# LSH attention with two gated layers: the first layer's weight rests all on GpSimd, two preparation parts a step at the start

## The chip, the cores and the metric

The kernel runs on one core of one Trainium2 chip. The metric is the device time of one execution in microseconds (us), median of several. The five engines are named as in the profile: PE (TensorE matmul; PEld its weight loads), DVE (VectorE), ACT (ScalarE), POOL (GpSimd), SP (SyncE, which here issues most DMAs).

## The reference

The computation is a masked attention, then two feed-forward layers, in fp32:

```
q_bits = (q @ proj > 0);  k_bits = (k @ proj > 0)          # 6 hash bits a token
mask   = bucket(q)[:, None] == bucket(k)[None, :]
scores = where(mask, scale * q @ k.T, -1e9)                # 2 batches, 8 heads, 768 tokens, 64 columns
x      = softmax(scores) @ v                               # -> (1536, 512)
x      = (silu(x @ w_gate) * (x @ w_val)) @ w_out          # first layer, d_ff 1536
h      = x @ w_in
out    = (max(h, 0) + alpha * min(h, 0)) @ w_out2          # second layer, d_ff 2048
```

The weights arrive as 64-bit numbers (raw blocks of 128x512, 512 KB each).

## The kernel before

**Precision.** Every operand of the layers is held as two rounded parts, a head (h) and a rest (l), and a product is three matmuls (lines 608 to 610). For a weight block this means: load the raw block (line 489, DMA issued by SP), make an fp32 block `wt` from it (`round64`: line 506 on ACT, 507 and 509 on DVE, 511 on POOL), round it to the head in `wb` (`w_h`, line 546, ACT), and subtract the head to get the rest (`w_l`, line 553). The rest of block i is made on POOL where i is even and on DVE where i is odd (`PL = (2, 1)`). The first layer has 36 blocks (24 of w_gate and w_val, 12 of w_out); they are new only in the first pass and are put into a scratch in DRAM after it (`w_put`, line 557, SP), from which later passes load both parts ready. So line 553 works for the first layer 36 times, 18 on each engine. The buffers of this pipeline: raw 2, `wr` 2, `wt` 3, `wb` 5.

**Attention.** It is cut into 24 items: a batch, a pair of heads, and a group of 256 queries. An item has two units, one per head. A unit goes through four parts: `banks` (score matmuls, lines 280 and 281, and their evacuation, 282), `top` (the maximum over keys, lines 286 to 289, and a transpose), `back` (the maximum broadcast, subtraction on DVE, line 307, and exponential on ACT, line 312) and `values` (matmuls of line 319). A unit yields 8 times, an item 16 times. Behind every one of these small pieces `step()` (line 380) pops one part from the list `todo`. The list holds the preparation of the next items (`prep`, line 223): for the first item of a pair of heads the rests of the keys (line 175, head 0 on POOL, head 1 on DVE), rounding of the queries (180) and their rest (183, POOL), two hashes of the keys and one of the queries. A hash is four matmuls (191, 192), the bits (197, DVE) and two copies into the operands (203, ACT). All hashes of the start pass through one PSUM tile `hp` and one SBUF tile `mk`. Before a unit's banks the list is emptied by force until its item is ready (line 435).

**Order.** At the start the attention runs alone until the first four items (one group of queries of all four head pairs) are done (line 791); in this time the loads and the first conversions of weights are called from `prime`. Then the pass `stage1(0)` of the first layer over these 256 tokens runs with the attention of the next group between its blocks, at two pieces per yield, and so on for three more groups; then a pass over 512 tokens, then three passes of the second layer. The lines of the source are a priority: the framework that places the instructions lets one whose inputs it takes to be late stand behind later ones, so the order on an engine is read from the trace.

```
        def step():
            if todo:
                todo.pop(0)()
...
            n, m = PL
            eng = nc.gpsimd if i % n < m else nc.vector
```

Of the kernel before, what the change touches and what calls it, by code (L numbers as in the profile page):

```python
# [46 lines left out]
def lsh_attention_moe_kernel(  # L47
# [12 lines left out]
    nc = tc.nc  # L60
# [8 lines left out]
    NPAIR = H // 2  # L69
# [11 lines left out]
    def f32(ap):  # L81
        return ap.bitcast(F32)
# [45 lines left out]
    at = Bag()  # L128
# [20 lines left out]
    def load_v(it):  # L149

        t = at.sm.tile([P, NC, 3 * D], F32, tag="vv", name="vv", bufs=4)
        VV[it.b, it.p] = t
        nc.gpsimd.memset(t[:, :, D:2 * D], 1.0)
        for x in range(2):
            nc.sync.dma_start(out=t[:, :, 2 * x * D:(2 * x + 1) * D], in_=vP[it.b, 2 * it.p + x])

    def load_k(it):

        if it.b == 0:
            it.nat = wp.tile([P, S], F32, tag="raw64", name="nat", bufs=RAWB)  # L160
        else:
            it.nat = at.sm.tile([P, S], F32, tag="nat", name="nat", bufs=1)
        nc.sync.dma_start(out=it.nat, in_=kview2(it))
        nc.gpsimd.dma_start(out=KA(it)[0:D], in_=kview(it))
        nc.gpsimd.dma_start(out=KB(it)[0:D], in_=kview(it))

    def load_q(it, eng=nc.sync):
        it.qr = at.sm.tile([P, 2, GQ], F32, tag="qr", name="qr", bufs=2)
        eng.dma_start(out=it.qr, in_=qview(it))
# [53 lines left out]
    def prep(it):  # L223

        def rest():
            pass

        todo = []
        if it.first:
            todo += [lambda x=x: rest_k(it, x, nc.gpsimd if POOL_K[x] else nc.vector) for x in range(2)]  # L230
        if it.first and it.b > 0:
            todo += [lambda: load_v(it)]
        todo += [lambda: round_q(it), lambda: rest_q(it)] + [rest] * (1 if it.first else 4)
        if it.first:
            todo += hash_k(it, 0) + hash_k(it, 1)
        todo += hash_q(it)
        last = todo[-1]

        def end():
            last()  # L240
            it.ready = True

        todo[-1] = end
        return todo

    def load(it):
        if it.first and it.b > 0:
            load_k(it)
        load_q(it)
# [7 lines left out]
    def first_item(it):  # L257
        ka, kb = KA(it), KB(it)
        for x in range(2):
            nc.scalar.activation(out=ka[0:D, x], in_=it.nat[x * D:(x + 1) * D, :], func=AF.Copy)  # L260
        round_q(it)
        for x in range(2):
            rest_k(it, x, nc.vector)
        nc.vector.tensor_tensor(out=it.QB[0:D], in0=it.qr[0:D], in1=f32(it.QA)[0:D], op=ALU.subtract)
        for x in range(2):
            nc.scalar.activation(out=kb[0:D, x], in_=it.nat[x * D:(x + 1) * D, :], func=AF.Copy)
        for fn in hash_q(it) + hash_k(it, 0, "G") + hash_k(it, 1, "G"):
            fn()
        it.ready = True

    def s_bank(u, j):
        it = u.it
        if j == 0:
            u.se = at.sm.tile([P, NC, GQ], F32, tag="se", name="se", bufs=at.nse)
        pt = at.ps.tile([P, 2, GQ], F32, tag=at.tag["S"][j], name="S", bufs=at.nb[at.tag["S"][j]])
        qa, qb = it.QA[:, u.x, :], it.QB[0:KR, u.x, :]
        ka, kb = KA(it)[:, u.x, :], KB(it)[0:KR, u.x, :]
        for i in range(2):
            sl = slice((2 * j + i) * P, (2 * j + i + 1) * P)
            nc.tensor.matmul(pt[:, i, :], lhsT=ka[:, sl], rhs=qa, start=True, stop=False)  # L280
            nc.tensor.matmul(pt[:, i, :], lhsT=kb[:, sl], rhs=qb, start=False, stop=True)  # L281
        nc.scalar.activation(out=u.se[:, 2 * j:2 * j + 2, :], in_=pt, func=AF.Copy)  # L282

    def s_max(u):
        m2 = at.sm.tile([P, 2, GQ], F32, tag="m2", name="m2", bufs=1)
        nc.vector.tensor_tensor(out=m2, in0=u.se[:, 0:2, :], in1=u.se[:, 2:4, :], op=ALU.max)
        nc.vector.scalar_tensor_tensor(out=m2, in0=u.se[:, 4:6, :], scalar=FLOOR, in1=m2, op0=ALU.max, op1=ALU.max)
        u.m1 = at.sm.tile([P, GQ], F32, tag="m1", name="m1", bufs=1)
        nc.vector.tensor_tensor(out=u.m1, in0=m2[:, 0, :], in1=m2[:, 1, :], op=ALU.max)

    def s_mt(u):

        tp = at.ps.tile([P, 2, P], F32, tag=at.tag["m"], name="mt", bufs=at.nb[at.tag["m"]])
        for j in range(2):
            nc.tensor.transpose(tp[:, j, :], u.m1[:, j * P:(j + 1) * P], ident)
        u.mq = at.sm.tile([P, 2, 1], F32, tag="mq", name="mq", bufs=2)
        nc.vector.tensor_reduce(out=u.mq, in_=tp, axis=AX.X, op=ALU.max)

    def s_mb(u):
        bc = at.ps.tile([P, 2, P], F32, tag=at.tag["m"], name="mb", bufs=at.nb[at.tag["m"]])  # L300
        for j in range(2):
            nc.tensor.transpose(bc[:, j, :], u.mq[:, j, :].to_broadcast([P, P]), ident)  # L302
        u.mx = bc.rearrange("p a b -> p (a b)")
# [7 lines left out]
    def s_exp(u):  # L311
        nc.scalar.activation(out=u.se, in_=u.se, func=AF.Exp, scale=SCALE)  # L312
# [39 lines left out]
    for b in range(B):  # L352
        order = [(p, g) for g in range(NG) for p in range(NPAIR)]
        for p, g in order:
# [3 lines left out]
            it.first = not any((o.b, o.p) == (b, p) for o in items)  # L358
            items.append(it)
    at.done = 0  # L360

    def attention():

        us = []
        for it in items:
            for x in range(2):
                u = Bag()
                u.it, u.x = it, x
                us.append(u)
        todo = []  # L370

        def queue(i):

            if i + 2 < len(items):
                todo.extend(prep(items[i + 2]))
            if i + 3 < len(items):
                n = 2 if items[i + 2].first and i > 0 else 1
                todo.insert(min(len(todo), n), lambda: load(items[i + 3]))

        def step():  # L380
            if todo:
                todo.pop(0)()

        load_k(items[1])
        load_q(items[1])
        load_v(items[0])
        first_item(items[0])
        for i in (2, 3):
            load_k(items[i])
            load_v(items[i - 1])  # L390
        load_q(items[2])
        load_v(items[3])
        todo.extend(prep(items[1]))

        def banks(u):
            for j in range(3):
                s_bank(u, j)
                step()
                yield
            if u.x == 1:  # L400
                queue(u.it.i)

        def top(u):
            s_max(u)
            s_mt(u)
            step()
            yield

        def back(u):
            s_mb(u)  # L410
            s_sub(u)
            s_exp(u)
            step()
            yield

        def values(u):
            for j in range(3):
                s_pv(u, j)
                if j == 2 and u.x == 1:
                    s_den(u.it)  # L420
                    s_out(u.it)
                    s_xh(u.it)
                    s_xl(u.it)
                step()
                yield

        order = []
        for i, u in enumerate(us):
            for k, part in enumerate((banks, top, back, values)):
                slot = i + LAGS[k]  # L430
                order.append(((slot, i, k) if slot < OLDER else (slot, k, i), part, u))
        order.sort(key=lambda o: o[0])
        for _, part, u in order:
            if part is banks:
                while not u.it.ready:
                    todo.pop(0)()
            yield from part(u)
# [3 lines left out]
    F2I = 3 * F1  # L441
# [27 lines left out]
    seq = order1() * (len(RATES) + 1) + o2 * NP2  # L469
# [78 lines left out]
    def w_l(i):  # L548

        if new[i]:  # L550
            n, m = PL
            eng = nc.gpsimd if i % n < m else nc.vector
            eng.tensor_tensor(out=ready[i][:, 1, :], in0=wt.pop(i), in1=f32(ready[i])[:, 0, :], op=ALU.subtract)  # L553

    def w_put(i):
# [216 lines left out]
    def more():  # L772

        if next(side, 0) == 0:
            kv.close()
            return False
        return True

    def prime(k):

        if k == 60:
            setup_alpha()
        k -= PRIME[0]
        if k >= 0 and k % PRIME[1] == 0:
            i = k // PRIME[1]
            upto("load", min(i, 7), w_load)
            if i >= 4:
                upto("conv", min(i - 3, 4), w_conv)

    k = 0  # L790
    while at.done < NPAIR:
        more()
        k += 1
        prime(k)
    at.tag = dict(S="SSM", m="S", hp="S", po="po")
    early_steps = w_early()
    ws.pin = False
# [78 lines left out]
```

## Time and profile before

| | us |
|---|---|
| median of 3 runs | 916.35 |
| lowest, highest | 914.65, 919.17 |
| profiled execution, whole | 920.38 |
| its span, first to last instruction | 918.60 |

| engine | busy us in the span | share |
|---|---|---|
| PE | 845.2 | 92% |
| DVE | 570.9 | 62% |
| ACT | 441.6 | 48% |
| POOL | 377.0 | 41% |

The shares are means over stages with different limits. The span falls, by what the engines do, into the attention alone (to about 73 us, where the first weight is converted), the pass in which the 36 blocks of the first layer are converted (73 to 250 us) and the rest, where PE works almost without a pause. The profiled execution took 4.03 us more than the median of the runs.

### The profile page before, as it was taken

Reading aid. Unit: us, or ns where it says so; the run is one execution under the profiler, and the core shown is the slowest. Engines: PE = TensorE matmul, PEld = TensorE weight load, DVE = VectorE, ACT = ScalarE, POOL = GpSimd, SP = SyncE. Lnnn points to the kernel's source line nnn. Section 1 sums busy time; section 2 is a strip of 40 time slices with the busy share of each in tenths; the row PEclk is TensorE's granted clock in tenths of the full one; section 3 lists DMA queues with packets and bytes.
Section 4 is the critical chain, followed back from the end, with each engine's and each line's share of the span. In section 5 each row is a group of like instructions: output and inputs, shape, how many; then the busy total and the mean of one; then the engine's idle time right before and its main releaser. Section 6 shows DMA issues by size and latency. Waiting matters only on the chain.

```text
span 918.6 us, 13016 instructions
## 1 busy us (share of the span) xinstructions
PE 845.2 (92%) x4816; PEld 737.4 (80%) x4816; DVE 570.9 (62%) x856; ACT 441.6 (48%) x760; POOL 377.0 (41%) x327
## 2 busy tenths in 40 slices
PE   5798778677899999999999999899999999999998
PEld 3577667566789999999999987687888888888886
DVE  5689997897847766778786537564543344335432
ACT  5578566646646566565665323231433343333331
POOL 4215565666514312223221235443454445444442
PEclk9999899989999999999999999999999999999999
DMA  9424567789899756776766698887300010001001
GB/s 216 101 70 147 195 233 251 235 223 281 260 342 307 209 190 211 243 237 226 247 220 213 227 341 299 318 299 277 136 1 1 1 47 0 1 1 46 1 0 46
DMA packets 63487, 158.45 MB, mean 172 GB/s; under 512 B 18112, under 2 KB 24256, under 8 KB 63424
## 3 DMA queue, kind: packets, MB, share of 16 engines
q1 hardware_dynamic: 61264, 152.07, 49.7%
q0 software_dynamic: 2016, 5.51, 2.9%
q8 instruction: 38, 0.62, 0.3%
q14 instruction: 25, 0.20, 0.1%
q10 hardware_dynamic: 144, 0.05, 0.0%
HBM read 132.44 MB, written 25.17 MB: 172 GB/s over the span
## 4 chain that ended last, share of the span: by engine, by line
PE 69%; DVE 12%; ACT 5%; DMA 5%; POOL 5%; issue 3%; SPq 0%; POOLq 0%; DVEq 0%; ACTq 0%
PE po L319 9%; PE gp L608 6%; PE gp L609 6%; PE gp L610 6%; PE op L614 5%; PE hp L609 5%; PE op L613 5%; PE hp L608 5%; PE op L615 5%; PE hp L610 5%; DMA wb<-w 3%; POOL wt L511 3%; PE yp L610 3%; PE yp L608 3%; PE yp L609 3%
## 5 line engine op out<-in xcount | busy, mean ns | idle before, releaser
L603 POOL TENSOR_TENSOR gl<-ex,gh 128x512 fp32r<-128x512 f32 (+1 forms) x108 | 116.6, 1079 | 220.9 <-ACT gh L600 162.7
L608 PE MATMUL gp<-xh,wb 128*128 128x256 f32 (+1 forms) x480 | 155.9, 325 | 22.2 <-ACT wb L546 12.1
L610 PE MATMUL gp<-xh,wb 128*128 128x256 f32 (+1 forms) x480 | 150.6, 314 | 7.4 <-DVE wb L553 3.8
L609 PE MATMUL gp<-xl,wb 128*128 128x256 f32 (+1 forms) x480 | 148.7, 310 | 1.7 <-POOL xl L348 1.7
L319 PE MATMUL po<-se,vv 128*128 128x256 f32 x576 | 145.7, 389 | 4.8 <-ACT se L312 3.9
L608 PEld LDWEIGHTS gp<-xh,wb 128*128 128x128 f32 x480 | 93.1, 194 | 33.4 <-ACT wb L546 15.1
L319 PEld LDWEIGHTS po<-se,vv 128*128 128x128 f32 x576 | 104.6, 194 | 18.5 <-ACT se L312 5.9
L546 ACT ACTIVATE wb<-w 128x512 fp32r<-128x512 f32 x96 | 60.7, 632 | 117.8 <-PE hp L610 78.9
L600 ACT ACTIVATE gh<-ex 128x512 fp32r<-128x512 f32 (+1 forms) x108 | 57.8, 535 | 109.0 <-DVE ex L597 46.7
L553 POOL TENSOR_TENSOR wb<-w,wb 128x512 fp32r<-128x512 f32 x48 | 62.1, 1294 | 110.3 <-ACT wb L546 108.3
L610 PEld LDWEIGHTS gp<-xh,wb 128*128 128x128 f32 x480 | 93.6, 195 | 14.1 <-DVE wb L553 5.1
L312 ACT ACTIVATE se<-se 128x1536 f32<-128x1536 f32 x48 | 71.3, 1485 | 61.6 <-DVE se L307 61.4
L609 PEld LDWEIGHTS gp<-xl,wb 128*128 128x128 f32 x480 | 93.7, 195 | 6.0 <-POOL xl L348 1.9
L553 DVE TENSOR_TENSOR wb<-w,wb 128x512 fp32r<-128x512 f32 x48 | 36.4, 758 | 91.5 <-ACT wb L546 91.5
L282 ACT ACTIVATE se<-S 128x512 f32<-128x512 f32 x144 | 80.2, 593 | 22.7 <-PE S L281 19.1
L511 POOL TENSOR_TENSOR wt<-wt,wr 128x512 int32<-128x512 int32 x48 | 67.7, 1410 | 54.7 <-DVE wt L509 29.8
L307 DVE SCALAR_TENSOR_TENSOR se<-se,mb 128x1536 f32<-128x1536 f32 x48 | 83.8, 1745 | 5.0 <-PE mb L302 4.7
L280 PE MATMUL S<-QA,kt 128*128 128x256 f32 x288 | 82.9, 317 | 2.5 <-ACT se L282 2.3
L608 PE MATMUL yp<-gh,wb 128*128 128x256 f32 (+1 forms) x240 | 76.0, 318 | 7.6 <-ACT wb L546 5.7
L281 PE MATMUL S<-qb,kt 76*128 76x256 f32 x288 | 75.8, 295 | 2.4 <-ACT kt L203 2.2
L610 PE MATMUL yp<-gh,wb 128*128 128x256 f32 (+1 forms) x240 | 72.6, 308 | 4.9 <-POOL wb L553 3.4
L608 PE MATMUL hp<-xh,wb 128*128 128x512 f32 x192 | 74.7, 389 | 0.0
(94 smaller groups left out, 1852.2 us busy)
## 6 DMA issues: line engine op xcount, KB each, us to landing
wb<-w SPq DMA_DIRECT2D x144, 512.0 KB, 4.6
raw<-in_wblk_dram SPq DMA_DIRECT2D x68, 512.0 KB, 4.2
w<-wb SPq DMA_DIRECT2D x36, 512.0 KB, 4.9
qr<-in_q_dram SPq DMA_DIRECT2D x24, 256.0 KB, 3.7
kt<-in_k_dram POOLq DMA_DIRECT2D x14, 384.0 KB, 9.3
nat<-in_k_dram SPq DMA_DIRECT2D x8, 384.0 KB, 5.0
vv<-in_v_dram SPq DMA_DIRECT2D x16, 192.0 KB, 6.7
whole<-wt SPq DMA_DIRECT2D x12, 256.0 KB, 2.2
```

What stands on the lines that cost most here:

```text
L280: nc.tensor.matmul(pt[:, i, :], lhsT=ka[:, sl], rhs=qa, start=True, stop=False)
L281: nc.tensor.matmul(pt[:, i, :], lhsT=kb[:, sl], rhs=qb, start=False, stop=True)
L282: nc.scalar.activation(out=u.se[:, 2 * j:2 * j + 2, :], in_=pt, func=AF.Copy)
L307: nc.vector.scalar_tensor_tensor(out=u.se, in0=u.se, scalar=FLOOR, in1=u.mx[:, None, :].to_broadcast([P, NC, GQ]), op0=ALU.max, op1=ALU.su ...
L312: nc.scalar.activation(out=u.se, in_=u.se, func=AF.Exp, scale=SCALE)
L319: nc.tensor.matmul(it.po[:, u.x, :], lhsT=VV[it.b, it.p][:, kb, u.x * D:u.x * D + P], rhs=u.se[:, kb, :], start=kb == 0, stop=kb == NC - 1)
L511: pin(nc.gpsimd.tensor_tensor(out=a, in0=a, in1=r, op=ALU.add))
L553: eng.tensor_tensor(out=ready[i][:, 1, :], in0=wt.pop(i), in1=f32(ready[i])[:, 0, :], op=ALU.subtract)
L603: nc.gpsimd.tensor_tensor(out=l, in0=ex, in1=f32(h), op=ALU.subtract)
L608: nc.tensor.matmul(pt, lhsT=h, rhs=ah, start=first, stop=False)
L609: nc.tensor.matmul(pt, lhsT=h, rhs=al_, start=False, stop=False)
L610: nc.tensor.matmul(pt, lhsT=l, rhs=ah, start=False, stop=last)
```

## The change

Two edits. First, the rests of all 36 new blocks of the first layer are made on POOL, not only those with even numbers (`seq[i] < F2I` holds for the first layer's blocks); the blocks of the second layer keep the alternation. Second, while `at.alone` is true `step()` pops two parts instead of one. It is true from the start until two items are done; the loop sets it anew before each piece.

```diff
@@ attention()
     at.done = 0
+    at.alone = True
...
         def step():
-            if todo:
-                todo.pop(0)()
+
+            for _ in range(2 if at.alone else 1):
+                if todo:
+                    todo.pop(0)()
@@ w_l(i)
             n, m = PL
-            eng = nc.gpsimd if i % n < m else nc.vector
+            eng = nc.gpsimd if i % n < m or seq[i] < F2I else nc.vector
             eng.tensor_tensor(out=ready[i][:, 1, :], in0=wt.pop(i), in1=f32(ready[i])[:, 0, :], op=ALU.subtract)
@@ the loop over the first four items
     while at.done < NPAIR:
+        at.alone = at.done < NPAIR - 2
         more()
         k += 1
         prime(k)
+    at.alone = False
```

## Rows read from the trace of the kernel before

**Rows 1.** Busy time by stretch: stretch, its length, busy us (instructions) of PE, PEld, DVE, ACT, POOL, clock, DMA.

```profile
31.00:46.00 15.00, 12.31 (x73) 9.09 (x71) 10.06 (x18) 11.36 (x22) 2.10 (x2) 1.00 0.06 18
46.00:61.00 15.00, 13.08 (x70) 10.56 (x69) 13.25 (x18) 10.64 (x18) 2.98 (x3) 0.89 0.31 105
61.00:73.00 12.00, 11.01 (x70) 9.45 (x69) 10.18 (x19) 11.18 (x20) 2.43 (x2) 1.00 0.08 23
...
73.00:250.00 177.00, 138.33 (x836) 119.76 (x835) 156.51 (x226) 108.69 (x191) 106.73 (x87) 0.93 0.72 230
...
250.00:300.00 50.00, 48.58 (x359) 45.69 (x358) 30.25 (x50) 25.16 (x48) 18.04 (x18) 1.00 1.02 322
```

**Rows 2.** DVE by line, 73 to 250 us: count, busy us, mean ns, idle before, releaser.

```profile
L509 DVE SCALAR_TENSOR_TENSOR wt<-raw,wt 128x512 int32<-128x512 int32 x36 | 30.8, 855 | 0.1
L507 DVE TENSOR_SCALAR wt<-raw 128x512 int32<-128x512 int32 x35 | 24.9, 711 | 0.1
L307 DVE SCALAR_TENSOR_TENSOR se<-se,mb 128x1536 f32<-128x1536 f32 x14 | 24.4, 1742 | 0.1
L553 DVE TENSOR_TENSOR wb<-wt,wb 128x512 fp32r<-128x512 f32 x18 | 19.0, 1058 | 10.1 <-ACT wb L546 9.9
L287 DVE SCALAR_TENSOR_TENSOR m<-se,m 128x512 f32<-128x512 f32 x14 | 14.3, 1021 | 0.1
L289 DVE TENSOR_TENSOR m<-m 128x256 f32<-128x256 f32 x14 | 12.2, 870 | 0.1
L286 DVE TENSOR_TENSOR m<-se 128x512 f32<-128x512 f32 x14 | 11.2, 797 | 2.5 <-ACT se L282 2.3
```

**Rows 3.** POOL by line, 73 to 250 us.

```profile
L511 POOL TENSOR_TENSOR wt<-wt,wr 128x512 int32<-128x512 int32 x36 | 50.8, 1411 | 44.7 <-DVE wt L509 28.6 <-ACT wr L506 6.4 <-ACT qb L203 2.8
L553 POOL TENSOR_TENSOR wb<-wt,wb 128x512 fp32r<-128x512 f32 x18 | 24.3, 1349 | 10.6 <-ACT wb L546 10.5
L603 POOL TENSOR_TENSOR gl<-ex,gh 128x256 fp32r<-128x256 f32 x12 | 11.1, 928 | 8.0 <-ACT gh L600 5.8 <-DVE wt L509 2.0
...
L348 POOL TENSOR_TENSOR xl<-xf,xh 128x256 fp32r<-128x256 f32 x7 | 6.3, 895 | 5.2 <-ACT xh L344 5.2
```

**Rows 4.** Single lines over the span: duration in ns as min/median/max, first and last start.

```profile
L509 DVE SCALAR_TENSOR_TENSOR wt<-raw,wt x48: 644/684/1773, 72.3 to 545.2; 128x512 int32<-128x512 int32 x48
...
L507 DVE TENSOR_SCALAR wt<-raw x48: 374/422/2729, 71.7 to 544.8; 128x512 int32<-128x512 int32 x48
...
L553 POOL TENSOR_TENSOR wb<-wt,wb x18: 1267/1284/1709, 75.2 to 244.8; 128x512 fp32r<-128x512 f32 x18
...
L553 DVE TENSOR_TENSOR wb<-wt,wb x18: 677/693/1735, 87.1 to 246.1; 128x512 fp32r<-128x512 f32 x18
...
L287 DVE SCALAR_TENSOR_TENSOR m<-se,m x48: 648/684/1801, 18.9 to 506.5; 128x512 f32<-128x512 f32 x48
...
L289 DVE TENSOR_TENSOR m<-m x48: 403/418/1870, 19.6 to 509.1; 128x256 f32<-128x256 f32 x48
...
L286 DVE TENSOR_TENSOR m<-se x48: 647/692/2139, 18.0 to 503.3; 128x512 f32<-128x512 f32 x48
```

**Rows 5.** Timeline, 160 to 168 us, DVE and POOL: start us, duration us, engine, line.

```profile
163.58 1.71 DVE L553 TENSOR_TENSOR wb<-wt,wb 128x512 fp32r<-128x512 f32 x1
...
163.47 1.27 POOL L511 TENSOR_TENSOR wt<-wt,wr 128x512 int32<-128x512 int32 x1 [0.69 <-ACT wb L546]
```

**Rows 6.** Waits, 73 to 250 us: who for whom, us in total, times, longest.

```profile
PE gp L608 <- ACT wb L546: 12.1, 13, 1.9
```

**Rows 7.** Timeline of PE, 30 to 49 us.

```profile
31.03 0.41 PE L191 MATMUL hp<-kt,skh 128*44 128x384 f32 x1
...
38.59 0.29 PE L281 MATMUL S<-qb,kt 76*128 76x256 f32 x1
...
46.45 0.38 PE L281 MATMUL S<-qb,kt 76*128 76x256 f32 x1 [0.15 <-ACT qb L203]
```

**Rows 8.** Chain that ended last within 30 to 62 us, its shares by line.

```profile
by line: ACT se L282 19.8%; ACT kt L203 16.4%; ACT se L312 13.9%; PE po L319 12.9%; issue 8.3%; DVE se L307 6.8%; ACT qb L203 3.9%; DVE mk L197 3.5%; PE S L281 3.0%; ACT den L325 2.4%; DVE m L286 2.2%; PE mb L302 2.1%; ACT QA L180 2.0%; DVE
```

## The prediction

> **What bounds the kernel now.** I read the stretches first, for what each one lacks. From 250 us on PE is busy 48.6 of 50 us, and nothing of the change lies there [rows 1]. Both edits work before that, where PE waits. From 73 to 250 us, the pass in which the weights are converted, DVE is busy 156.5 of 177 us and POOL 106.7 [rows 1]; PE's recorded 138.3 is inflated by the modelled ends, and it waits for weight heads again and again (12.1 us at the gate matmuls alone [rows 6]). So this stretch is set by the conversion and its engines, DVE and POOL. From 31 to 61 us, in the attention alone, no engine is full: in 30 us DVE has 23.3, ACT 22.0, PE 25.4 [rows 1]. A chain that passes from engine to engine sets this part.
>
> I then read DVE and POOL by line and compared each mean with the same line's median over the whole span, which is what it takes undisturbed. On DVE the means are far above the medians exactly on the lines that read two operands in SBUF, and on line 507; line 307, which reads one in SBUF and one in PSUM, is steady at 1.742 us [rows 2, 4]. One pair shows why: DVE's line 553 starts at 163.58 us while a POOL subtraction or addition runs from 163.47 to 164.74, and takes 1.71 us instead of 0.693: it ends 0.55 us behind POOL's end [rows 4, 5]. These DVE lines and the POOL instructions take turns. I call the time lost so a stall. It sums to 36 x (0.855 - 0.684) + 35 x (0.711 - 0.422) + 18 x (1.058 - 0.693) + 14 x (1.021 - 0.684) + 14 x (0.870 - 0.418) + 14 x (0.797 - 0.692) = 35.4 us over 131 instructions, 0.27 us each [rows 2, 4].
>
> **Edit 1, the rests on POOL.** It removes 18 instructions from DVE, 19.0 us with their stalls, 12.5 us undisturbed (18 x 0.693), and the 10.1 us for which DVE stood before them, waiting for the head from ACT with all its other work queued behind [rows 2, 4]. It adds 18 to POOL at 1.349 us, 24.3 us, each of which waits for the same head, at 10.6 us for the 18 that are there now [rows 3]. Queued behind such a wait on POOL are the next block's addition (line 511), for which ACT's rounding and then PE wait, and the rests of the gates (line 603).
>
> Seen from DVE alone: POOL's work grows to 131.0 us. If a stall grows with POOL's share of the time, at a stretch of 160 us it is 0.27 x (131.0 / 160) / (106.7 / 177) = 0.367 us, over 113 remaining instructions 41.4 us. DVE then has 156.5 - 35.4 - 12.5 + 41.4 = 150.0 us of work and 20.5 - 10.1 = 10.4 us of other idling: 160.4 us, a gain of 16.6.
>
> Seen from POOL alone: 131.0 us, its waits for gate heads (8.0) and for line 344 (5.2), and its waits for weight heads, 10.6 us if the new ones fall into time that POOL lost anyway, 21.2 if they double [rows 3]. That is 154.8 to 165.4 us, if of the 44.7 us that it now stands before line 511 nothing remains. But 28.6 of these are waits for DVE's line 509 [rows 3], and shrink only as far as DVE gets ahead, for which there are three `wt` buffers and two raw ones.
>
> Seen from the turns: POOL's 106.7 us and the undisturbed time of the DVE lines that take turns, 36 x 0.684 + 35 x 0.422 + 18 x 0.693 + 14 x (0.684 + 0.418 + 0.692) = 77.0 us, make 183.7 us in a stretch of 177 (records overlap where one hands over to the next) [rows 1, 2, 4]. The edit takes 12.5 from this and adds 24.3. By this sum it loses 11.8 x 177 / 183.7 = 11.4 us. What it can win back is that more of the work that needs no turn (line 307 alone is 24.4 us [rows 2]) comes to lie over POOL's, and that DVE is no longer held up before the rests.
>
> So the ends are -16.6 and +11.4. I take -4, somewhat beyond their middle (-2.6), since POOL's own sum leaves at least 11.6 us of room (177 - 165.4) and DVE is the engine that is full.
>
> The rule that speaks against the edit is in the Trainium skill, "SBUF — State Buffer", section "Who interferes with whom": a DVE instruction with two inputs in SBUF and a GpSimd instruction that reads SBUF exclude each other, and the one that comes second stands until the first is done. The pair at 163.5 us agrees with it (1.71 us against 0.693) [rows 4, 5]. Taken strictly it makes the third sum the right one.
>
> The store of a block (line 557) waits on SP for the rest, with the next raw load behind it. If the rest is later by a POOL instruction, so is that load. I cost this at nothing, since DVE never stands before line 507 (0.1 us) [rows 2]; without that cover a load late by 1.3 us would cost up to that much a block. The new wait of line 507 for a `wt` buffer that POOL, not DVE, sets free has the same cover: three buffers.
>
> **Edit 2, two parts a step.** No instruction is added or removed. By counting pops in the source: the 14 parts of item 1 are done behind the last bank of unit 1, where now six pops are forced before unit 2; those of item 2 at the end of unit 0's values, where now they end with unit 2's entry into `back`; those of item 3 behind the last bank of unit 4, not by force behind unit 5's. The query loads move with them by one or two pieces on SP, with two `qr` buffers and nothing urgent behind them.
>
> What it can bring is bounded by the chain from 30 to 62 us: the copies of the hash bits on ACT (16.4% and 3.9%) and the bits on DVE (3.5%) are 23.8% of 32 us, 7.6 us [rows 8]. The score matmuls of item 2 start at 46.45 us on the last of its copies [rows 7]: earlier preparation starts them earlier. But pops are only a priority: the first hash of item 1 runs on PE at 31.03 us, behind score and value matmuls that the source has later [rows 7], so item 1, whose score matmuls resume at 38.59 us [rows 7], is held by data or its estimate, not by the count of pops. DVE's idle time from 31 to 61 us, 6.7 us [rows 1], is the other limit. I take -3, between 0 and -6.7. A loss comes about if a hash or a key rest stands before a unit's own work; its bound is about one hash with its bits and copies, 2.6 us (two hashes' worth of copies lie no further apart in the chain: (38.59 - 31.03) / 3 = 2.5) [rows 7]. What is saved here reaches the start of the weight pass: the stretch from 61 to 73 us has ACT at 11.2 of 12 us [rows 1] and shifts as a whole.
>
> **The sum.** Profiled execution: 920.38 us, its span 918.60 and 1.78 around it. -4 and -3 give 913.4. That execution is 4.03 above the median of the runs, so the median becomes 916.35 - 7 = 909.3.
>
> **The rivals.**
> - *The turns decide* (slower). Place: 73 to 250 us. Price: +11.4 us, less the 3 of edit 2: 924.7 us. It decides from the point at which DVE's work that needs no turn no longer finds POOL's to lie over. For it: the sum of turns already exceeds the stretch. Against it: DVE's 10.1 us before line 553, which turns do not explain.
> - *The gain is hidden* (no change). DVE's relief goes into more stalls and POOL's queue delays the head of the next block, about as much as DVE is ahead; edit 2 only changes priorities that the framework overrides. 915.5 us, with 1 us from edit 2. For it: the three sums cancel nearly (-16.6 and +11.4), and PE's first hash at 31.03 us.
> - *DVE alone is the bound* (much faster). POOL's waits before line 511 take in the rests: -16.6 and -4: 895.7 us. For it: DVE's 88% share; against it: POOL's share would be 82% in a queue in order.
>
> **How the numbers follow.** The forecast (about 902 to 911.5) has a chance of 0.45, DVE alone 0.07, no change 0.25, the turns 0.23. What a measurement here can tell from no change is 0.5%, 4.6 us. Faster 0.52, same 0.26, slower 0.22. The range 898 to 925 takes in the turns' price and leaves out the fastest end and a loss beyond it.
>
> **What would show it.** Line 553 gone from DVE in the stretch and 36 times on POOL; the stretch near 173 us; stalls near 0.35 us an instruction; POOL's 44.7 us before line 511 down by more than 20. For edit 2: score matmuls of item 2 before 45 us, ACT's first conversion (line 506) some 3 us sooner. I am wrong if POOL is busy over 85% of the stretch and DVE's lines 507 and 509 have means over 1 us (the turns), or if the conversion starts later than now.

## The result, and the profile after

The changed kernel takes 927.93 us, the median of 7 runs (923.73 to 930.56). Against the kernel before on the same chip this is a ratio of 1.0114 [1.009, 1.0139]: slower by about 1.1%, where I had forecast 909.3 and a range that ended at 925. The profiled execution took 930.56 us with a span of 928.7, the highest of its runs, as that of before was 4.03 above its median; the two traces differ by 10.2 us, the medians by 11.6. In the listing after the change the lines from 381 on stand three further down: 506 is now 509, 507 is 510, 509 is 512, 511 is 514, 546 is 549, 553 is 556, 608 and 610 are 611 and 613.

Where the 10.2 us lie is read from the first and the last matmul of the first pass. In the timeline of PE before, the columns being start us, us, engine, line and operation, these are

```profile
89.14 0.39 PE L608 MATMUL gp<-xh,wb 128*128 128x256 f32 x1
...
248.54 0.28 PE L610 MATMUL yp<-gh,wb 128*128 128x256 f32 x1
```

and after:

```profile
88.16 0.38 PE L611 MATMUL gp<-xh,wb 128*128 128x256 f32 x1 [0.50 <-DVE mq L297]
...
256.55 0.28 PE L613 MATMUL yp<-gh,wb 128*128 128x256 f32 x1
```

The pass begins 1.0 us sooner and ends 8.0 us later: 168.4 us instead of 159.4. The second pass then ends at 359.1 us instead of 349.2, 9.9 later, and the rest of the kernel takes as long as before.

The two kinds of lost time in the pass are seen in its busy time by engine. The columns are the stretch, its length, then busy us and instructions of PE, PEld, DVE, ACT and POOL, granted clock, DMA share and GB/s. Before:

```profile
89.10:248.50 159.40, 122.70 (x745) 105.99 (x745) 140.22 (x200) 95.36 (x169) 98.90 (x81) 0.94 0.75 238
...
195.00:255.00 60.00, 47.94 (x302) 40.59 (x302) 47.68 (x73) 35.39 (x63) 37.41 (x33) 0.97 0.87 265
```

After, with the stretch of [rows 1], and with 73 to 195 and 195 to 255 us:

```profile
88.20:256.50 168.30, 129.42 (x757) 112.29 (x758) 142.79 (x183) 94.51 (x167) 123.19 (x98) 0.89 0.72 227
...
73.00:250.00 177.00, 134.64 (x781) 116.10 (x779) 151.40 (x195) 102.32 (x180) 128.25 (x100) 0.89 0.68 219
73.00:195.00 122.00, 91.50 (x561) 78.34 (x559) 113.42 (x145) 75.33 (x132) 91.36 (x70) 0.96 0.66 219
195.00:255.00 60.00, 47.35 (x249) 41.20 (x250) 42.83 (x58) 30.36 (x54) 41.22 (x35) 0.77 0.75 222
```

PE's recorded busy time in the pass grew by 6.7 us for nearly the same matmuls (757 against 745), its idle time by 2.2 (from 36.7 to 38.9). The first goes with the clock: its mean fell from 0.94 to 0.89, which over these lengths is 9.6 us of full clock lost before and 18.5 after. Both kinds lie in the last third: from 195 to 255 us PE got through 249 matmuls instead of 302 in the same 60 us, at a clock of 0.77 instead of 0.97. (Of the 60 us before, the last 6.5 already belong to the second pass.)

The lines of [rows 2] and [rows 3] are found again after. DVE from 73 to 250 us (count, busy us, mean ns, idle before, releaser):

```profile
L510 DVE TENSOR_SCALAR wt<-raw 128x512 int32<-128x512 int32 x35 | 35.1, 1003 | 0.2
L512 DVE SCALAR_TENSOR_TENSOR wt<-raw,wt 128x512 int32<-128x512 int32 x36 | 33.0, 916 | 0.3
L307 DVE SCALAR_TENSOR_TENSOR se<-se,mb 128x1536 f32<-128x1536 f32 x12 | 20.9, 1743 | 0.3 <-PE mb L302 0.3
L286 DVE TENSOR_TENSOR m<-se 128x512 f32<-128x512 f32 x12 | 15.2, 1262 | 0.3
L287 DVE SCALAR_TENSOR_TENSOR m<-se,m 128x512 f32<-128x512 f32 x13 | 13.8, 1065 | 0.3
L289 DVE TENSOR_TENSOR m<-m 128x256 f32<-128x256 f32 x13 | 13.6, 1045 | 0.1
```

and POOL:

```profile
L556 POOL TENSOR_TENSOR wb<-wt,wb 128x512 fp32r<-128x512 f32 x34 | 49.5, 1457 | 15.7 <-ACT wb L549 15.5
L514 POOL TENSOR_TENSOR wt<-wt,wr 128x512 int32<-128x512 int32 x35 | 48.8, 1394 | 22.5 <-DVE wt L512 20.4 <-ACT wb L549 1.4 <-DMA w<-wb 0.7
```

DVE lost the 18 rests and is still busy 151.4 us: every line that takes turns with POOL became longer, line 510 from 711 to 1003 ns, line 286 from 797 to 1262, while line 307 stayed at 1743. Against the medians of [rows 4] the stalls are 36 x (0.916 - 0.684) + 35 x (1.003 - 0.422) + 12 x (1.262 - 0.692) + 13 x (1.065 - 0.684) + 13 x (1.045 - 0.418) = 48.6 us over 109 instructions, 0.446 us each, against 0.27 before. POOL's idle time before its addition fell from 44.7 to 22.5 us, so it did take in the rests, but a rest now takes 1.457 us on the mean, where it took 1.349 [rows 3], and 1.284 undisturbed: POOL stands too. And the additions come later. Worked out from the two traces, the addition of a block starts 0.77 us on the mean behind the end of what it needs (lines 509 and 512), 27.6 us over the 36 blocks; before it was 0.37 and 13.4 us.

What PE waits for from 90 to 255 us (us in total, times, longest) changed accordingly. Before:

```profile
PE gp L608 <- ACT wb L546: 12.1, 13, 1.9
PE yp L608 <- ACT wb L546: 5.7, 9, 1.6
PE gp L610 <- DVE wb L553: 3.8, 4, 2.1
PE gp L610 <- POOL wb L553: 3.5, 6, 1.0
PE yp L610 <- POOL wb L553: 3.4, 5, 0.9
...
PE yp L610 <- DVE wb L553: 1.5, 2, 1.0
```

After:

```profile
PE gp L613 <- POOL wb L556: 14.4, 15, 2.2
PE gp L611 <- ACT wb L549: 9.1, 8, 2.3
PE yp L613 <- POOL wb L556: 6.1, 6, 2.0
PE yp L611 <- ACT wb L549: 2.4, 5, 0.7
```

Waits for rests rose from 12.2 to 20.5 us, waits for heads fell from 17.8 to 11.5. The longest stand of a rest, at 210 us after, in the timelines of DVE, POOL and PE:

```profile
209.53 0.68 DVE L286 TENSOR_TENSOR m<-se 128x512 f32<-128x512 f32 x1
210.13 0.68 DVE L512 SCALAR_TENSOR_TENSOR wt<-raw,wt 128x512 int32<-128x512 int32 x1
210.74 0.67 DVE L287 SCALAR_TENSOR_TENSOR m<-se,m 128x512 f32<-128x512 f32 x1
211.45 1.37 DVE L289 TENSOR_TENSOR m<-m 128x256 f32<-128x256 f32 x1
...
209.83 2.70 POOL L556 TENSOR_TENSOR wb<-wt,wb 128x512 fp32r<-128x512 f32 x1 [0.74 <-ACT wb L549]
...
212.59 0.58 PE L613 MATMUL gp<-xh,wb 128*128 128x256 f32 x1 [1.85 <-POOL wb L556]
212.97 0.41 PE L611 MATMUL gp<-xh,wb 128*128 128x256 f32 x1
213.18 0.41 PE L612 MATMUL gp<-xl,wb 128*128 128x256 f32 x1
```

POOL stands 0.74 us for the head, DVE's line 286 begins in that time, and then lines 286, 512 and 287 run one behind the other at their undisturbed durations while POOL's rest stands: it takes 2.70 us instead of 1.28. PE stands 1.85 us for it, and the matmuls behind take 0.41 us, at the lower of the clock's two levels (1.2 GHz), where the same ones take 0.28 at the higher (2.4 GHz). Rest late, PE idle, clock down. But this pair is no picture of the usual rest: of the 36 it is the only one over 2 us, the next takes 1.74, the median is 1.30. The 18 rests that came straight behind a wait for their head took 1.47 us on the mean, the other 18 took 1.43.

### The profile page after: what moved, and what is told of

The parts are those of the page before. It is cut to its first block, busy times and chain, and to the rows that moved or that the text cites. A ratio compares the mean times of both kernels' runs of the same rounds, so it can differ in the third digit from the quotient of the medians.

```text
span 928.7 us, 13055 instructions
## 1 busy us (share of the span) xinstructions
PE 849.8 (92%) x4816; PEld 741.4 (80%) x4816; DVE 574.6 (62%) x838; ACT 441.0 (47%) x760; POOL 402.8 (43%) x345
## 4 chain that ended last, share of the span: by engine, by line
PE 68%; DVE 9%; POOL 6%; DMA 5%; issue 3%; ACT 3%; SPq 0%; POOLq 0%; DVEq 0%; ACTq 0%
PE po L319 8%; PE gp L613 6%; PE gp L611 6%; PE gp L612 6%; PE op L616 5%; PE hp L611 5%; PE op L618 5%; PE hp L613 5%; PE hp L612 5%; PE op L617 5%; PE yp L613 3%; DMA wb<-w 3%; PE yp L611 3%; PE yp L612 3%; POOL wt L514 3%
## 5 line engine op out<-in xcount | busy, mean ns | idle before, releaser
L606 POOL TENSOR_TENSOR gl<-ex,gh 128x512 fp32r<-128x512 f32 (+1 forms) x108 | 118.5, 1097 | 214.9 <-ACT gh L603 167.2
L611 PE MATMUL gp<-xh,wb 128*128 128x256 f32 (+1 forms) x480 | 158.7, 331 | 17.3 <-ACT wb L549 9.1
L613 PE MATMUL gp<-xh,wb 128*128 128x256 f32 (+1 forms) x480 | 152.1, 317 | 14.4 <-POOL wb L556 14.4
L611 PEld LDWEIGHTS gp<-xh,wb 128*128 128x128 f32 x480 | 94.9, 198 | 27.7 <-ACT wb L549 12.3
L613 PEld LDWEIGHTS gp<-xh,wb 128*128 128x128 f32 x480 | 95.1, 198 | 23.0 <-POOL wb L556 19.0
L514 POOL TENSOR_TENSOR wt<-wt,wr 128x512 int32<-128x512 int32 x48 | 66.9, 1394 | 33.7 <-DVE wt L512 21.6
```

The source lines that it names most:

```text
L514: pin(nc.gpsimd.tensor_tensor(out=a, in0=a, in1=r, op=ALU.add))
L606: nc.gpsimd.tensor_tensor(out=l, in0=ex, in1=f32(h), op=ALU.subtract)
L611: nc.tensor.matmul(pt, lhsT=h, rhs=ah, start=first, stop=False)
L613: nc.tensor.matmul(pt, lhsT=l, rhs=ah, start=False, stop=last)
```

## The experiments

My theory after the result: the moved rests lose by the turns. A rest reads two operands in SBUF, on POOL for 1.28 us instead of 0.69 on DVE, and in that time neither engine gets on with such work. The rivals: POOL's queue in order (it is held by the wait for the head, with the additions behind it), POOL's mere load, the second edit, and PE's clock by itself. All ratios are against the kernel before on the same chip; "pass" is from the first gate matmul to the last output matmul of the first pass, "idle" its length less PE's busy time, both from one profiled execution. A pass of one execution is good to some 5 us: before and edit 2 alone have the same rests on the same engines, and their passes differ by 4.6 us where their medians differ by 1 to 2. The runs lie on four chips. The kernel before has 916.35 us beside after, 915.58 beside edit 1 alone, edit 2 alone, 30 rests and memsets, 917.29 beside all on DVE, both turn and wait kernels and the filling matmuls, and 916.08 beside the earlier head and the late keys, so a difference of medians across chips can be off by 1 to 2 us.

| kernel | median us | ratio | pass us | PE busy / idle | clock |
|---|---|---|---|---|---|
| before | 916.35 | | 159.4 | 122.7 / 36.7 | 0.94 |
| after | 927.93 | 1.0114 [1.009, 1.0139] | 168.4 | 129.4 / 38.9 | 0.89 |
| edit 1 alone | 929.95 | 1.0158 [1.0131, 1.0186] | 171.6 | 131.3 / 40.3 | 0.88 |
| edit 2 alone | 914.53 | 0.9986 [0.9967, 1.0005] | 154.8 | 119.3 / 35.4 | 0.96 |
| 30 rests on POOL | 919.54 | 1.0043 [1.0017, 1.0069] | 161.2 | 124.6 / 36.6 | 0.92 |
| rests as memsets | 915.12 | 1.0000 [0.9981, 1.002] | 154.8 | 118.8 / 36.0 | 0.94 |
| all rests on DVE | 914.71 | 0.997 [0.9938, 1.0003] | 151.6 | 122.3 / 29.3 | 0.91 |
| wait, no turn | 914.13 | 0.9957 [0.9931, 0.9984] | 154.1 | 121.5 / 32.6 | 0.93 |
| turn, no wait | 919.38 | 1.0013 [0.9994, 1.0033] | 160.1 | 125.7 / 34.4 | 0.94 |
| filling matmuls | 928.08 | 1.0108 [1.0062, 1.0154] | 159.8 | 128.3 / 31.5 | 0.89 |
| head a block earlier | 924.21 | 1.0099 [1.0068, 1.013] | 165.7 | 126.0 / 39.7 | 0.92 |

**Which edit.** Edit 1 alone:

```diff
-            for _ in range(2 if at.alone else 1):
+            for _ in range(1):
```

> Edit 1 alone: all rests of the first layer's new blocks on GpSimd, one part a step. If edit 1 does the harm and edit 2 gains the 1 to 2 us by which the changed kernel's first items are ahead at 73 to 98 us, this is slower than before by 12 to 14 us (about 929). If edit 2's other order does the harm later on, this is within 4 us of before, or faster.

Edit 2 alone:

```diff
-            eng = nc.gpsimd if i % n < m or seq[i] < F2I else nc.vector
+            eng = nc.gpsimd if i % n < m else nc.vector
```

> Edit 2 alone: two parts a step, the rests alternate as before. If edit 1 does the harm: 1 to 3 us faster than before (about 914). If edit 2 does it: 8 to 12 us slower. If the two only harm together: no change here and none with edit 1 alone.

Edit 1 alone is slower than before by 14.4 us of median, and after is slower than edit 2 alone by 13.4, or 11.7 by the ratios, since these two ran on different chips. The whole loss is edit 1's. Edit 2's gain of 1.1 us can't be told from no change.

DVE's stalls do not measure this loss. DVE from 73 to 250 us in edit 2 alone, then in edit 1 alone:

```profile
L512 DVE SCALAR_TENSOR_TENSOR wt<-raw,wt 128x512 int32<-128x512 int32 x35 | 34.0, 972 | 0.1
L510 DVE TENSOR_SCALAR wt<-raw 128x512 int32<-128x512 int32 x35 | 27.3, 780 | 0.1
L287 DVE SCALAR_TENSOR_TENSOR m<-se,m 128x512 f32<-128x512 f32 x14 | 18.2, 1302 | 0.2
...
L512 DVE SCALAR_TENSOR_TENSOR wt<-raw,wt 128x512 int32<-128x512 int32 x35 | 31.6, 902 | 0.2
L510 DVE TENSOR_SCALAR wt<-raw 128x512 int32<-128x512 int32 x35 | 29.4, 841 | 0.2
L287 DVE SCALAR_TENSOR_TENSOR m<-se,m 128x512 f32<-128x512 f32 x13 | 16.7, 1286 | 3.5 <-ACT se L282 3.2
```

Summed as above, the stalls are 44.5 us in edit 2 alone (0.342 us an instruction), which is no slower than before with its 35.4, and 41.0 us in edit 1 alone (0.376), which loses 14.

**How much for how many rests.** With both edits, the first 24 rests and then every second one on POOL, 30 in all:

```diff
-            eng = nc.gpsimd if i % n < m or seq[i] < F2I else nc.vector
+            eng = nc.gpsimd if i % n < m or i < 24 else nc.vector
```

> Both edits, but only the first 24 of the 36 blocks have all their rests on GpSimd; the last 12 alternate as before. In the trace of the changed kernel the stretch from 73 to 195 us is ahead of before by 3 us, and 9 us are lost from 195 to 255. If the loss belongs to the last blocks (there the next pass's loads and the next batch's keys come in), this is 1 to 4 us faster than before. If the turns of DVE and GpSimd cost evenly at each of the 18 moved rests, it is two thirds of the way: 6 to 9 us slower. If the clock's fall is an event that comes by chance of the order, it may lie anywhere between, and the granted clock of 195 to 255 us tells it.

919.54 us: 5.0 above edit 2 alone, on the same chip, for 12 more rests, 0.42 us each; the last 6 cost the other 8.4, or 6.5 by the ratios. So the loss is not made in the last part alone, though there it is dearer.

**All rests on DVE.** The opposite of the change, with edit 2:

```diff
-            eng = nc.gpsimd if i % n < m or seq[i] < F2I else nc.vector
+            eng = nc.gpsimd if i % n < m and seq[i] >= F2I else nc.vector
```

> Both edits, but the other way round: the first layer's 36 rests all on DVE, none on GpSimd. If the turns of DVE and GpSimd are what bounds the conversion, this is the cheapest use of them (0.69 us a rest in place of 1.28 us): 5 to 10 us faster than two parts a step alone (914.5), about 906. If DVE's own time is the bound, 18 more instructions of 0.69 us and their waits for the head cost 10 to 25 us: 925 to 940. Between both, if the alternation is a balance.

If DVE's own time set the pass, 18 more rests on it would have cost at least 12.5 us. They cost nothing: 914.71 us against the 914.53 of edit 2 alone, and a pass of 151.6. But if the turns were the whole bound, this kernel should have won about as much as the change lost (I expected 5 to 10 us), and it won nothing either. DVE from 73 to 250 us in this kernel, the rest's line, and the busy time of the stretch:

```profile
L556 DVE TENSOR_TENSOR wb<-wt,wb 128x512 fp32r<-128x512 f32 x36 | 33.0, 919 | 2.4 <-ACT wb L549 1.9
...
73.00:250.00 177.00, 145.16 (x889) 126.00 (x890) 169.08 (x246) 109.39 (x193) 87.22 (x72) 0.92 0.77 253
```

DVE is busy 169.1 of 177 us and stands 2.4 us before its 36 rests, where it stood 10.1 us before 18 [rows 2]; PE got through 889 matmuls in the stretch, against 836 [rows 1], though here 13 us of it lie behind the end of the pass. DVE at 88% was not full in the sense in which I had taken it. The median does not follow the pass, because the shorter pass holds less work: 290 of the attention's matmuls fall into it, where 312 did in edit 2 alone, and the other 22 come in the second pass, which takes 106.3 us instead of 100.2. Both passes together take 257.9 us, against 255.0. From 250 to 260 us PE is busy 7.22 of 10 us in this kernel, and DVE stands in front of a key rest:

```profile
249.43 0.42 DVE L594 SCALAR_TENSOR_TENSOR ex<-ex,gp 128x256 f32<-128x256 f32 x1
254.99 0.95 DVE L175 TENSOR_TENSOR kt<-nat,kt 64x768 fp32r<-64x768 f32 x1 [5.14 <-DMA nat<-in_k_dram]
```

**Rests that read nothing.** In the next three the 18 moved rests do not give the rest: they are replaced, and those parts of the weights are left out of the result. First, two memsets to zero on POOL, which write, read nothing and wait for no head:

```diff
-            eng.tensor_tensor(out=ready[i][:, 1, :], in0=wt.pop(i), in1=f32(ready[i])[:, 0, :], op=ALU.subtract)
+            if seq[i] < F2I and i % n >= m:
+                wt.pop(i)
+                for _ in range(2):
+                    nc.gpsimd.memset(f32(ready[i])[:, 1, :], 0.0)
+            else:
+                eng.tensor_tensor(out=ready[i][:, 1, :], in0=wt.pop(i), in1=f32(ready[i])[:, 0, :], op=ALU.subtract)
```

> Both edits, but each of the 18 moved rests is two memsets to zero on GpSimd instead of the subtraction (so these rests are left out of the products): it takes GpSimd's time and its place in the queue, still writes the tile, but reads nothing from SBUF and no longer waits for the head. If the turns with DVE cost the time: stalls of DVE's two-input lines fall back to 0.3 us or less an instruction, and the time is 5 to 15 us below before. If it is GpSimd's queue in order and its load: within 4 us of the changed kernel's 928.

915.12 us and a pass of 154.8: the loss is gone, though POOL is busy 121.7 us from 73 to 250 us, against 128.3. So POOL's busy time by itself does not cost it. Two of my signs failed, though: the time is that of before and not 5 to 15 us below it, and DVE's stalls are 0.381 us an instruction, not 0.3 or less. That a memset does not hold up an instruction with two operands shows in single places. DVE and POOL at 84 us, then at 96 us, in this kernel:

```profile
84.65 0.69 DVE L286 TENSOR_TENSOR m<-se 128x512 f32<-128x512 f32 x1
...
84.21 1.11 POOL L559 MEMSET wb<- 128x512 f32 x2
...
96.37 0.86 DVE L510 TENSOR_SCALAR wt<-raw 128x512 int32<-128x512 int32 x1
...
95.84 1.10 POOL L559 MEMSET wb<- 128x512 f32 x2
```

Line 286 lies almost wholly beside two memsets and takes its undisturbed 0.69 us. Line 510, which has one operand, takes 0.86 us instead of 0.42. And wait and turn went together in this run.

**Wait without turn.** The moved rest makes its first 32 columns properly, and so waits for the head, and two memsets take the place of the other 480 columns:

```diff
+            if seq[i] < F2I and i % n >= m:
+                t = wt.pop(i)
+                eng.tensor_tensor(out=ready[i][:, 1, 0:32], in0=t[:, 0:32], in1=f32(ready[i])[:, 0, 0:32], op=ALU.subtract)
+                for _ in range(2):
+                    nc.gpsimd.memset(f32(ready[i])[:, 1, 32:512], 0.0)
+            else:
                 eng.tensor_tensor(...)
```

> Both edits, but each of the 18 moved rests is cut to its first 32 columns, followed by two memsets of the other 480 on GpSimd (the rests' other columns are left out): GpSimd still waits for the head and is busy about as long, but reads SBUF only shortly. If the turns with DVE cost the time: 913 to 918, as with memsets alone (915.1). If GpSimd's wait for the head, with its queue in order behind, costs it: 924 to 930.

**Turn without wait.** The moved rest is `wt - wt`, of the same shape and with two operands in SBUF, but it needs no head:

```diff
+            if seq[i] < F2I and i % n >= m:
+                t = wt.pop(i)
+                eng.tensor_tensor(out=ready[i][:, 1, :], in0=t, in1=t, op=ALU.subtract)
+            else:
                 eng.tensor_tensor(...)
```

> Both edits, but each of the 18 moved rests is, on GpSimd, the fp32 block minus itself (so it is left out): the same two-operand instruction of 1.28 us, but it needs no head from ScalarE. If the turns cost the time: 924 to 930, as the changed kernel. If the wait for the head does: 913 to 918.

POOL and DVE by line in the kernel that waits and takes hardly a turn, 73 to 250 us, and its stretch:

```profile
L562 POOL TENSOR_TENSOR wb<-wt,wb 128x512 fp32r<-128x512 f32 x18 | 24.6, 1368 | 2.2 <-ACT wb L549 2.2
L560 POOL MEMSET wb<- 128x480 f32 x36 | 18.2, 505 | 0.6
L558 POOL TENSOR_TENSOR wb<-wt,wb 128x32 fp32r<-128x32 f32 x18 | 7.8, 434 | 4.5 <-ACT wb L549 4.4
...
L510 DVE TENSOR_SCALAR wt<-raw 128x512 int32<-128x512 int32 x35 | 21.0, 601 | 3.0 <-DMA raw<-in_wblk_dram 2.7
...
73.00:250.00 177.00, 140.99 (x873) 123.51 (x874) 148.20 (x211) 107.64 (x194) 128.13 (x143) 0.94 0.73 245
```

A replaced rest takes 0.434 + 2 x 0.505 = 1.44 us, as a true one did (1.457), and POOL is busy 128.13 us against 128.25. The time is 914.13, 13.8 us below after. But only the 32 columns are bound to the head: 31 of the 36 memsets started before their block's head was done, and behind the head POOL has 0.31 us of work (the median of line 558) instead of 1.3. So POOL's waits for heads sum to 4.5 + 2.2 us instead of 15.7, and the additions start 0.34 us behind what they need, 12.4 us in all, instead of 0.77 and 27.6. The run shows that POOL's load and a short wait for the head cost nothing. It takes away the reads and the queueing behind the head together, and so does not tell them apart.

The turn without the wait took 919.38 us, 5.3 above the wait without the turn on the same chip and with POOL as busy (126.3 us). So a moved rest that reads does cost, about 5 us for the 18, even where it waits for no head. That is less than half of what turn and wait cost together (13.4 us of median, 11.7 by the ratios), and lies between the two times that I had expected. In this kernel DVE's stalls (0.425 us an instruction) and the queueing of the additions (21.6 us) are almost those of after, but 15 of the 18 moved rests start before their head is done. PE's waits for heads and rests together go with the times: 26.1 us in edit 2 alone, 26.4 with the wait alone, 28.9 with the turn alone, 32.0 after. So the whole loss needs both: a rest that reads, and one that stands behind its head. How the two work together is open. That a rest behind a wait has to stand for a whole run of DVE, as at 210 us, is not it: only that one did. Nor is it lateness alone: with all rests on DVE a rest ended 2.43 us behind its head on the mean, after 2.26.

**The head a block earlier.** If the wait makes the turn dearer, an earlier head should give something back. After, with load, conversion and head of the first pass one block ahead:

```diff
-        upto("h", n + LEAD[1], w_h)
+        d = 1 if n < 3 * F1 - 8 else 0
+        upto("h", n + LEAD[1] + d, w_h)
...
-        upto("conv", n + LEAD[2], w_conv)
-        while ws.load < min(NWT, n + (LEAD[3] if fresh[min(ws.load, NWT - 1)] else LEAD[2])):
+        upto("conv", n + LEAD[2] + d, w_conv)
+        while ws.load < min(NWT, n + (LEAD[3] + d if fresh[min(ws.load, NWT - 1)] else LEAD[2])):
```

> The changed kernel with load, conversion and head of the first pass's blocks called one block earlier, the rest where it was. So far: the turn without the wait for the head costs 5 us (919.4 against 914.5), the wait without the turn nothing (914.1), both together 13. If the rest on GpSimd costs more because it waits behind its own addition for ScalarE's head, with GpSimd's queue standing, an earlier head takes the wait away and 916 to 922 us remain. If the load of turns alone makes it, 925 to 932.

924.21 us, 3.7 below after by the medians and 1.4 by the ratios, whose intervals overlap: no gain is shown. The edit took away only a part of the wait: POOL stood 10.6 us before its rests for heads, against 15.7.

**The clock by itself.** After, with 8 matmuls with zero weights added to each of the 24 gate and value blocks of the first pass, so that PE has something to do around its waits:

```diff
+        fresh_pass = ws.used <= 3 * F1
+        for j in range(4 if fresh_pass else 0):
+            nc.tensor.matmul(pt, lhsT=zw, rhs=xh[:, 0, :], start=n == 0 and j == 0, stop=False)
...
+            for j in range(4 if fresh_pass and kk == 0 else 0):
+                nc.tensor.matmul(pt, lhsT=zw, rhs=ah, start=False, stop=False)
```

> The changed kernel with 8 matmuls of zero weights added to each of the 24 gate and value blocks of the first pass, 4 ahead of the block and 4 ahead of the first matmul with its rest, where TensorE waits; they add nothing to the result and cost 192 x 0.118 = 23 us of TensorE at full clock, partly within its waits. In the traces so far the length of the first pass goes with the time at the lower clock, at about 0.5 us for each us. If the fall of the clock in TensorE's waits is what makes the loss, the time at the lower clock from 73 to 255 us falls from 38 to under 15 us and the kernel to 915 to 922. If the waits cost as such, with the clock only their sign: 928 to 940.

928.08 us. The mean clock in the pass stayed at 0.89: the fillers did not hold it up, so the run does not tell what the clock costs by itself. The pass was 8.6 us shorter in the profile, the whole was not: without the 192 fillers the pass holds 682 matmuls, where after has 757, and what it left of the attention came in the second pass, which took 109.3 us instead of 102.5. This test failed, and the question stays open.

**After the gain of the pass.** Three kernels tried to keep what a shorter pass wins by putting the key rests of the second batch four parts later: with edit 2 alone, with all rests on DVE, and with every third rest on POOL.

```diff
-        if it.first:
-            todo += [lambda x=x: rest_k(it, x, nc.gpsimd if POOL_K[x] else nc.vector) for x in range(2)]
+        keys = [lambda x=x: rest_k(it, x, nc.gpsimd if POOL_K[x] else nc.vector) for x in range(2)]
+        if it.first and it.b == 0:
+            todo += keys
...
+        if it.first and it.b > 0:
+            todo += keys
```

> Two parts a step alone (rests alternate), and in the second batch the rests of the keys come four parts later in the preparation. A control for the next one: within 3 us of 914.5.

> All 36 rests on DVE, and the second batch's key rests four parts later. With the rests on DVE the first pass is 3 us shorter than with the alternation (151.6 us against 154.8), but the second pass lost 9 us, where DVE stands 5.1 us before a key rest for its DMA. If that stand is what takes the gain back, this is 5 to 8 us faster than 914.7: 907 to 910. If the loads have only come nearer together and the DMA queues are the limit, no change.

> 12 of the 36 rests on GpSimd, 24 on DVE, and the second batch's key rests four parts later. By the number of rests on GpSimd the stretch from first to last head is 156.3 (0), 162.1 (18), 168.3 (30) and 174.6 us (36), about 0.5 us a rest: 160 us here. 908 to 914 us, between the two others.

| rests on POOL, keys late | median us | ratio | pass us |
|---|---|---|---|
| 18 of 36 | 914.78 | 0.9989 [0.997, 1.0008] | 155.1 |
| none | 913.43 | 0.9974 [0.9952, 0.9995] | 151.1 |
| 12 of 36 | 915.93 | 1.0009 [0.999, 1.0027] | 159.7 |

With none on POOL, DVE stands 4.8 us for ACT at the place where it stood for the keys, the second pass ends at 343.6 us as it did without the delay (343.3), and the ratio of 0.9974 lies within what I call no change. The delay is worth nothing. The third row is a miss: 12 rests on POOL did not come out between none and 18. It is 2.5 us above none on the same chip, more than the spread of the runs leaves open, so from 18 rests downwards the times do not go by the number of rests.

## Why the prediction was wrong

**What bounds the kernel.** That the pass from 73 to 250 us is set by the conversion on DVE and POOL held. That "DVE is the engine that is full" did not: its 156.5 us held 35.4 us of standing for POOL [rows 2, 4], which I had counted myself, and with all 36 rests on DVE the kernel did not become slower. A busy share that holds standing time is not a load.

**Edit 1: the step that failed** is the choice of -4 "somewhat beyond their middle" between three sums that contradict each other. They are not three estimates of one thing, whose middle means something: each assumes a different bound, and at most one can be right. The sum of the turns gave +11.4 us; the runs gave +11.7 to +13.4 (after against edit 2 alone) and +14.4 (edit 1 alone against before). It had already said that POOL's and DVE's work in turns, 183.7 us, filled a stretch of 177 [rows 1, 2, 4], and it was the only one of the three that counted what is shared. The two reasons for -4 failed. POOL's room of 11.6 us supposed that nothing was left of its 44.7 us before the additions; 22.5 us were left, and though POOL was busy only 128.25 of 177 us, the additions queued longer (27.6 us against 13.4). That DVE was full did not hold, as said. DVE's stand before its rests did vanish with them, but PE's stand for rests grew from 12.2 to 20.5 us. The run with 32 columns and memsets shows what it was not: with POOL as busy, but hardly reading and with little to do behind the head, the loss is gone.

The rule that I cited from the Trainium skill ("SBUF — State Buffer", "Who interferes with whom") agrees with the pairs at 163.5 us before and at 210 us after. So does its other half: the section says that a GpSimd instruction that only writes SBUF does not exclude DVE's two-input ones, and line 286 took 0.69 us beside two memsets. 36 memsets in place of nearly all of 18 rests took 13.8 us off (18 instructions of 32 columns still read), though they also freed POOL's queue.

**Its terms.** The stall per DVE instruction was to grow from 0.27 to 0.367 us with POOL's share of the time; it was 0.446 after, but 0.376 in edit 1 alone and 0.342 in edit 2 alone, where POOL's work is that of before: it does not go by POOL's share. POOL's side of the turn was missing: a rest there takes 1.457 us on the mean, not the 1.349 of [rows 3] that I used. And one thing is in none of the sums: PE's waits went with a lower granted clock, and 6.7 of the 9.0 us by which the pass grew are in PE's busy time, 2.2 in its idle time. So the third sum came near in size without holding the way by which the loss reaches PE. For the opposite move it gives a gain of the same 11.4 us, and none came; for the turn without the wait it gives most of the loss (18 x 1.161, the mean of the replaced rests, less 12.5 is 8.4 us), and under half came. That it came near here is in part luck.

**The waits.** I costed the store and the next raw load at nothing. That held: line 510 stands 0.2 us after, and the longer means there are turns, not loads. The additions queued behind POOL's rests I had named, and given no term of their own. They queued 13.4 us before, 10.5 in edit 2 alone, 25.1 in edit 1 alone and 27.6 after. In the kernel that waits and hardly reads this fell to 12.4 us, together with the reads, so no run shows what it costs apart from them.

**Edit 2.** Taken at -3, between 0 and -6.7; the runs gave -1.1, with an interval of -3.0 to +0.5 us. ACT's first conversion came 2.2 us sooner in the profile (line 509 at 69.36 us, line 506 at 71.57 before), but 1.3 of this also in the kernel without edit 2 (70.23). The score matmuls of item 2 resume at 46.78 us where they did at 46.45 [rows 7]: item 2 did not come earlier, as I had feared when I noted that pops are only a priority. So the end at nothing was nearer the truth than -3, and the rival in which the gain is hidden had its price of 1 us for edit 2 right.

**The rivals and the signs.** "The turns decide" (924.7 us, chance 0.23) came nearest, within 3.2 us, and holds in part: the reads count, but they make the whole loss only with the wait for the head. Its point of decision, work that needs no turn finding no more of POOL's to lie over, was not tested apart. My signs for it were set too high: POOL over 85% of the stretch, where it is at 72%, and both lines of the conversion on DVE over 1 us, where line 510 has a mean of 1003 ns and line 512 of 916. The loss came with POOL's share well below one.

**What stays open.** How much of the loss would go if the clock had stayed up; why wait and turn together cost 12 to 13 us where apart they cost about 5 and nothing; how much of it is the additions' queueing on POOL, for which a rest of full length behind its head that reads nothing would be needed; and what sets the time from 18 rests on POOL downwards, where fewer turns brought nothing (one stand of 5.14 us for keys is shown above, but taking it away brought nothing).

## What to carry to other kernels

Before moving an operation from VectorE to GpSimd, list the instructions of both that lengthen when they overlap, sum their undisturbed durations over the stretch, and compare with its length: if they fill it, expect the move to cost, however idle GpSimd looks. Here the difference of the two durations is 0.59 us a rest and the loss was 0.65 to 0.75; but take the sum as a warning and not as a price, since the opposite move won nothing. Look, too, at what stands in GpSimd's queue behind an instruction that waits. Take the standing time out of an engine's busy share before calling it full. And when two sums for one edit differ by 28 us, don't average them: find which of them counts the resource that the others leave out.

## What the runs showed of the hardware

- The turns go both ways. DVE's two-operand instructions stood for POOL's (a mean stall of 0.446 us after, 0.342 in edit 2 alone), and once a rest on POOL stood for three DVE instructions in a row (2.70 us instead of 1.28): at 210 us it did not get in between them.
- Line 510, a shift and mask with a single tensor operand in SBUF, takes turns as well: a median of 422 ns [rows 4], a mean of 1003 after, and of 876 and 601 in the two kernels with memsets. It took 0.86 us at 96 us beside memsets alone, where line 286, with two operands, kept its 0.69 us at 84 us.
- A POOL memset of 128x480 took 505 ns on the mean of 36, and 18.2 us of them beside a busy DVE cost the kernel no time.
- More and longer waits of PE went with a granted clock of 0.77 over 60 us, where it was 0.97 before, and with 249 matmuls instead of 302. Eight zero-weight matmuls a block did not hold the clock up.
